# The opening's last block, the plan of the weight forms and the ring of x forms in a fused attention and two-layer MoE kernel

## The chip, the cores and the metric

One core of one Trainium2 chip. The metric is device microseconds of one execution of the whole kernel. The matrix engine (PE in the profile) multiplies 128x128 tiles by 384 columns; VectorE is DVE, ScalarE is ACT, GpSimd is POOL, and SP issues nearly all DMAs.

## What is computed

A linear attention without softmax, a feed-forward layer with ELU, and a mixture of four ReLU experts weighted by given probabilities, all in float32:

```python
kv = einsum('bhsd,bhse->bhde', k, v); o = einsum('bhsd,bhde->bhse', q, kv)
x = o / sqrt(mean(o*o) + 1e-6) * g_norm          # (2304 tokens, 512)
h = x @ w_in                                     # (2304, 2048)
x = where(h > 0, h, exp(min(h, 0)) - 1) @ w_out  # (2304, 512)
out = sum_e p[:, e] * (relu(x @ w1[e]) @ w2[e])  # 4 experts, 512 -> 1024 -> 512
```

w_in and w_out arrive as float64 words. Every product is made of three matmuls of a high and a low part (hi*hi, hi*lo, lo*hi), so each operand must be split first: ACT casts the high part (L194, L321, L266, L638), and POOL or DVE subtracts it from the source for the low part (`split_lo` at L182, `finish_low` at L269).

## The kernel before, in words

The 2304 tokens are six blocks of 384 (`T`), numbered j = 0 to 5. d_ff of layer one is cut into 16 chunks in five groups (`first_groups`): chunks 0-1, 2-3, 4-7, 8-11, 12-15.

**Opening.** Attention and the first group (chunks 0 and 1) are planned by `at_place(place, op)`; the operations are sorted by place, and `in_program_order` (L796) fixes that order on PE, DVE, ACT and POOL. Per block there are two `product1` (x by w_in, 12 matmuls each, into PSUM banks a and b), `begin_elu` (ACT, L490-L491), `end_elu` (DVE, L495), `split_h` (ACT L194, POOL L191), then `half(j, ms)` (L529: x by w_out for two of the four output tiles m, 12 matmuls, into banks e and f) and `half_acc` (two ACT copies, L505, into the accumulator). The halves of block j-1 are placed inside block j; those of the last block stand alone at z = 120 to 123 (L867-L871).

**Rest of layer one.** 84 steps (one per group, block and chunk) run in a pipeline of half-steps, `hh`: on an even one `product1` of step s, then pending accumulations, `split_h` of step s-1 and the planned work of that half-step; on an odd one `emit_mm2` of step s-2 (`LAG = 2`, L1015; 12 matmuls), `begin_elu` and `end_elu` of step s, with the planned work between. For the first two odd half-steps there is no `emit_mm2`. Here the order is fixed on DVE, ACT and POOL alone; PE's is the scheduler's. In each group the weights of the next are converted from float64 and split. Their tiles come from the pools `w` (6 buffers) and `wl` (10 buffers of 4 KB per partition, L91).

**Weight forms.** Layer two multiplies by a scheme of seven products of half-size blocks (P1 to P7), so every quarter of an expert's weights is turned into seven forms, each split in two and written to DRAM (`keptw`) to be streamed later. For one quarter, `make_w` (L252) loads four blocks (b11 to b22), makes four sums on DVE (t1 to t4, L261) and seven splits: ACT cast (L266), one tick later the low part (L271, POOL, or DVE for the names in `late["on_vector"]`), one tick later the write by SP. Each form holds a 4 KB tile from the ring `f` from its sum or cast until the write has landed. Sixteen quarters exist; twelve are made in layer one. `plan_forms` (L292) puts each at half-step offsets out of `FORMS_SLOW` (L288, a new quarter every 16 half-steps, the first six from half-step 28) and `FORMS_FAST` (every 7, six more from half-step 124). From half-step 127 (L1011) P2 and P7 go to DVE, and the ring `f` takes its tiles in turn from its own pool `wf` (4 buffers, L984) and from `wl`: four and three of every seven. The last group begins at half-step 120. In it also the x forms of block pair 0 are made (half-steps 141 to 170).

**Layer two.** Three pairs of blocks by four experts are twelve moves of 14 slots. A slot is one unit of the first product ("q", PSUM qa/qb) of this move and one of the second ("m", ma/mb) of the move before, 12 matmuls each; a q unit reads one weight form and one x form. `evict_q` (L598) takes a q result away: u = ps + P1 (L604, DVE) after P3, for example, without which P5 can't reuse bank qb. A pair needs seven x forms, [128, 2, 2, 384] high and low, made by `make_forms` (L314) in eight calls: two sums; A11; S2; A12 and a sum; S1; S4 and a sum; S3; A22. Each form is an ACT cast (L321) and a tick later its low part (L191, in two pieces on POOL for A11, A12, S4 and A22; on DVE for S2, S1 and S3 of pairs 1 and 2). A form is read twice in a move: in the order A11, S2, A12, S1, S4, S3, A22 at slots 0 to 6 and again at slots 7 to 13. The eight calls for the next pair are made at slots 8 to 15 of a pair's last move (L1070; slot 14 is the next move's first). Forms lie two to a tile of pool `x` (4 buffers); a tile is taken anew for every two forms (`new_form`, L306). The sums take two tiles of pool `s` (16 buffers), which layer two uses for all its intermediate results.

Of the kernel before, what the change touches and what calls it, by code (L numbers as in the profile page):

```python
# [9 lines left out]
F32R = mybir.dt.float32r  # L10
# [23 lines left out]
def attention_moe_kernel(  # L34
# [15 lines left out]
    P = 128  # L50
# [14 lines left out]
    T = 384  # L65
    TT = T // P
    NB = NT // T
# [19 lines left out]
    layer1, with_x_late, with_wm = ExitStack(), ExitStack(), ExitStack()  # L87
    psum = layer1.enter_context(tc.tile_pool(name="psum", bufs=1, space=bass.MemoryType.PSUM))
    x_p = ctx.enter_context(tc.tile_pool(name="x", bufs=4))
    raw_p = layer1.enter_context(tc.tile_pool(name="raw", bufs=2, side="right"))  # L90
    wl_p = layer1.enter_context(tc.tile_pool(name="wl", bufs=10, side="right"))  # L91
    cv_p = layer1.enter_context(tc.tile_pool(name="cv", bufs=2, side="right"))
    h1_p = layer1.enter_context(tc.tile_pool(name="h1", bufs=4, side="right"))
    e_p = layer1.enter_context(tc.tile_pool(name="e", bufs=2, side="right"))
# [1 line left out]
    late = {"on_vector": ()}  # L96
# [3 lines left out]
    def bank(tags, name):  # L100

        n = turns[tags] = turns.get(tags, -1) + 1
        return psum.tile([P, 512], F32, tag=tags[n % len(tags)], name=name, bufs=1)
# [107 lines left out]
    wf = {}  # L211
# [73 lines left out]
        }  # L285


    FORMS_SLOW = "t1:0 t2:2 P5:3 t3:4 t4:6 P3:7 b12:8 b11:8 P4:9 P7:10 b22:10 P1:11 P2:13 b21:14 P6:15", 16  # L288
    FORMS_FAST = "t1:0 t2:1 P5:2 t3:2 b12:3 b11:3 b22:3 t4:3 P3:4 P4:4 P7:5 P1:5 P2:6 P6:7 b21:8", 7
    FORMS_LATE = "t1:0 t2:4 P5:5 t4:8 P3:9 t3:12 P7:13 b12:14 P4:16 P1:18 P2:20 P6:22 b11:22 b22:25 b21:25", 28  # L290

    def plan_forms(n, at, plan, put):  # L292
        steps = make_w(n)
        for what in plan[0].split():
            name, offset = what.split(":")
            if name[0] != "b" or n + 1 != IN_LAYER1:
                put(at + int(offset), steps[name])
        return at + plan[1]

    F_ORDER = [A_OF[q] for q in Q_ORDER]  # L300
    forms, halves = {}, {}
# [3 lines left out]

    def new_form(p, name):  # L306

        n = F_ORDER.index(name)
        if n % 2 == 0:
            halves[p, n] = x_p.tile([P, 2, 2, 2, T], F32R, tag="x", name="f")  # L310
        forms[p][name] = halves[p, n - n % 2][:, n % 2]
        return forms[p][name]

    def make_forms(p):  # L314
# [40 lines left out]
    at = ExitStack()  # L355
# [114 lines left out]
    banks2 = {}  # L470
# [46 lines left out]
    def emit_mm2(g, j, c):  # L517

        first, last = c == first_groups[g][0], c == first_groups[g][-1]
        if first:  # L520
            banks2[j] = [bank("efghcd", "ps_y")[:, :T] for _ in range(KD)]
        for m, ps in enumerate(banks2[j]):
            product2(ps, j, c, m, first, last)
        if last:
            pending.extend((g, j, m, ps) for m, ps in enumerate(banks2[j]))

    pending = []

    def half(j, ms):  # L529

        if j not in acc:
            new_acc(j, [P, KD, T])
        cs = first_groups[0]
        for m in ms:
            banks2[j, m] = bank("ef", "ps_y")[:, :T]
        for c in cs:
            for m in ms:
                product2(banks2[j, m], j, c, m, c == cs[0], c == cs[-1])
# [225 lines left out]
    def at_place(place, op, *args):  # L764
        plan.append((place, len(plan), op, args))
# [67 lines left out]
    for j in range(NB):  # L833
        z = 20 * j
# [29 lines left out]
    plan_float32(0, 3, 68.9, 71.6, 69, 73.9, 74)  # L864
    plan_float32(1, 2, 100, 100.1, 100.2, 103, 103.1)
    plan_float32(1, 3, 108.9, 109, 109.1, 114, 114.6)
    z = 20 * NB  # L867
    at_place(z, half, NB - 1, (0, 1))
    at_place(z + 1, half_acc, NB - 1, (0, 1))
    at_place(z + 2, half, NB - 1, (2, 3))  # L870
    at_place(z + 3, half_acc, NB - 1, (2, 3))  # L871


    for place, what in ((-31, "k0-1 w1c0 k2-4 q0-2 w1c1"), (-18.5, "k5-8 q3-5 w2c0"), (0, "w2c1 k9-11"), (0.05, "q6-8"),
# [95 lines left out]
    def at_step(hs_, *op):  # L970
        todo.setdefault(hs_, []).append(op)

    for g, cs in list(enumerate(first_groups))[1:]:
        begins = 2 * len(steps)
        for n, j in enumerate(range(NB) if g != 3 else range(NB)[::-1]):
            here = 2 * len(steps)
            if g == 1:
                at_step(here + 2, keep_x, j)
            elif g == 2 and n == 0:
                at_step(here, with_x_late.close)  # L980
                at_step(here, lambda: late.update(
                    b=[(with_wm.enter_context(tc.tile_pool(name="wm", bufs=4, reuse_waits="tile")), "b")] * 2 +
                      [(layer1.enter_context(tc.tile_pool(name="wm2", bufs=2, side="right", reuse_waits="tile")), "b")],
                    f=[(layer1.enter_context(tc.tile_pool(name="wf", bufs=4, side="right", reuse_waits="tile")), "f")],  # L984
                ))
                for b in ("b12", "b11", "b22", "b21"):
                    at_step(here, load_block, 0, b)
            if g >= 2 and n >= 4:
                at_step(here - 4 * len(cs), load_x, j)
            steps += [(g, j, c) for c in cs]  # L990
        length = 2 * len(steps) - begins
        if g + 1 < len(first_groups):
            cs = first_groups[g + 1]
            pieces = [p for i in range(0, len(cs), 2) for p in ((0, cs[i]), (0, cs[i + 1]), (1, cs[i]), (1, cs[i + 1]))]
            for n, row in enumerate(pieces):
                at_step(begins + n * (3 if g == 1 else 6), convert, len(rows))
                rows.append(row)
# [9 lines left out]
        at_step(begins + hh, make_one, forms_of_0)  # L1007
    at = begins - 2 * NB * NF * 2 + 4
    for n in range(IN_LAYER1):
        at = plan_forms(n, at, FORMS_SLOW if n < 6 else FORMS_FAST, lambda hh, step: at_step(hh, *step))  # L1010
    at_step(begins + 7, lambda: late.update(  # L1011
        on_vector=("P2", "P7"), f=[late["f"][0], (wl_p, "w")] * 3 + [late["f"][0]]
    ))

    LAG = 2  # L1015
    for hh in range(2 * (len(steps) + LAG)):
        s, second = divmod(hh, 2)
        if not second:
            if s < len(steps):
                product1(*steps[s][1:])  # L1020
            while pending:
                into_acc(*pending.pop(0))
            if 0 < s <= len(steps):
                split_h(*steps[s - 1][1:], nc.vector if s >= len(steps) - 2 else nc.gpsimd)
            tick(*todo.get(hh, ()))
        else:
            if s >= LAG:
                emit_mm2(*steps[s - LAG])
            if s < len(steps):
                begin_elu(*steps[s][1:])  # L1030
            tick(*todo.get(hh, ()))
            if s < len(steps):
                end_elu(*steps[s][1:])
# [33 lines left out]
    slots = len(M_UNITS)  # L1067
    for n, pair_end in enumerate(range(E, len(moves), E)):
        of_next = make_forms(n + 1)
        for slot in range(8, 16):  # L1070
            starts.setdefault(((pair_end - 1) * slots + slot) * 2 + 1, []).append((make_one, of_next))
    starts[0] = [(load_block, IN_LAYER1, b) for b in ("b12", "b11", "b22", "b21")]
    at = 4
    for n in range(IN_LAYER1, len(quarters)):
        at = plan_forms(n, at, FORMS_LATE, lambda half, step: starts.setdefault(half, []).append(step))
# [83 lines left out]
```

## Time and profile before

| | us |
|---|---|
| median of 3 runs | 1217.87 (1217.45 to 1218.7) |
| the profiled execution, its own time | 1217.92 |
| its span in the trace | 1216.1 |
| PE matmul busy in the span | 1175.8 |
| DVE, POOL, ACT busy | 795.5, 659.5, 587.1 |
| granted PE clock, mean of the span | 0.991 |

The span is 1.8 us shorter than the execution's own time, and that time is 0.05 us above the median. In the trace, time runs from the span's start. The opening ends at about 117 us; layer one then runs to 478 us and layer two to the end. A matmul's row may be longer than the distance to the next, since matmuls are pipelined; the number of matmuls in a stretch tells more than the busy time.

### The profile page before, as it was taken

The page shows a single profiled execution, that of the slowest core. Times are in us where ns is not written, and L with a number is a line of the kernel's source. Part 1 is how long each engine was busy: PE and PEld are TensorE (multiplying, and loading weights), DVE is VectorE, ACT ScalarE, POOL GpSimd, SP SyncE. Part 2 cuts the span into 40 slices and gives each one's busy share as a digit, 9 for nine tenths or more (in the row PEclk, how much of TensorE's full clock was granted, in tenths as well). Part 3 has the DMA queues.
Part 4 walks back from the last instruction along what each step waited for, and adds up shares of the span by engine and source line. Part 5 has one row for each costly group of instructions (what it writes and reads, how often), then busy time and mean ns, then how long its engine had stood idle before and what let it go on. Part 6 is the DMA issues. An engine that isn't in the chain of part 4 may idle for free.

```text
span 1216.1 us, 18927 instructions
## 1 busy us (share of the span) xinstructions
PE 1175.8 (97%) x7039; PEld 1157.4 (95%) x7039; DVE 795.5 (65%) x951; ACT 587.1 (48%) x937; POOL 659.5 (54%) x520
## 2 busy tenths in 40 slices
PE   8898999999999998999999999999999999999997
PEld 8798999999999988999999899999999999999996
DVE  5776896676764676477677956454758564647485
ACT  3666665665655564544444533433335334343432
POOL 1122446767656696576666955354447543544441
PEclk9999999999999999999999989999999999999999
DMA  9942247647678978999999868878887778787873
GB/s 344 351 153 106 88 153 244 211 157 268 221 176 291 351 278 324 324 340 362 314 357 324 308 238 260 274 246 271 253 268 236 244 256 278 245 275 254 265 244 115
DMA packets 112159, 312.22 MB, mean 257 GB/s; under 512 B 19580, under 2 KB 40644, under 8 KB 110532
## 3 DMA queue, kind: packets, MB, share of 16 engines
q1 hardware_dynamic: 107236, 306.30, 74.2%
q10 hardware_dynamic: 4832, 4.72, 1.2%
q8 instruction: 56, 0.92, 0.3%
q14 instruction: 35, 0.29, 0.1%
HBM read 238.06 MB, written 72.91 MB: 256 GB/s over the span
## 4 chain that ended last, share of the span: by engine, by line
PE 52%; DVE 4%; issue 1%; POOL 1%; DMA 1%; ACT 1%; ACTq 0%; DVEq 0%; POOLq 0%
PE ps_qb L576 15%; PE ps_ma L576 14%; PE ps_mb L576 11%; PE ps_qa L576 10%; DMA ws<-keptw 1%; DVE acc L685 1%; DVE m L684 1%; DVE f L191 1%; PE ps_mb L731 0%; POOL c L707 0%; DVE h L191 0%; POOL h L191 0%; DVE h L629 0%; DVE h L628 0%; DVE u L604 0%
## 5 line engine op out<-in xcount | busy, mean ns | idle before, releaser
L191 POOL TENSOR_TENSOR h<-h 128x384 fp32r<-128x384 f32 x232 | 280.2, 1232 | 212.4 <-ACT h L638 206.1
L576 PE MATMUL ps_qb<-f,ws 128*128 128x384 f32 x1152 | 218.7, 338 | 10.6 <-DVE u L604 9.5
L576 PEld LDWEIGHTS ps_qb<-f,ws 128*128 128x128 f32 x1152 | 202.7, 190 | 11.9 <-DVE u L604 10.5
L576 PE MATMUL ps_ma<-h,ws 128*128 128x384 f32 x1080 | 200.0, 335 | 0.8 <-DVE h L191 0.7
L191 POOL TENSOR_TENSOR h<-e,h 128x384 fp32r<-128x384 f32 x91 | 102.9, 1131 | 172.0 <-ACT h L194 160.1
L576 PEld LDWEIGHTS ps_ma<-h,ws 128*128 128x128 f32 x1080 | 187.9, 188 | 1.8 <-DVE h L191 1.0
L576 PE MATMUL ps_mb<-h,ws 128*128 128x384 f32 x936 | 174.3, 337 | 1.6 <-ACT o L738 0.8
L638 ACT CAST h<-h 128x768 fp32r<-128x768 f32 x168 | 139.9, 833 | 72.3 <-PE ps_ma L576 37.2
L576 PEld LDWEIGHTS ps_mb<-h,ws 128*128 128x128 f32 x936 | 165.1, 190 | 2.2 <-issue 1.1
L576 PE MATMUL ps_qa<-f,ws 128*128 128x384 f32 x864 | 163.0, 335 | 1.6 <-DMA ws<-keptw 1.0
L576 PEld LDWEIGHTS ps_qa<-f,ws 128*128 128x128 f32 x864 | 150.7, 188 | 2.5 <-issue 1.6
L481 PE MATMUL ps_h<-x,w 128*128 128x384 f32 x384 | 130.5, 340 | 7.6 <-DVE e L495 7.6
L595 ACT ACTIVATE h<-h 128x768 f32<-128x768 f32 x72 | 61.0, 847 | 152.9 <-DVE h L610 71.9
L514 PE MATMUL ps_y<-h,w 128*128 128x384 f32 x384 | 128.8, 335 | 1.7 <-POOL h L191 1.7
L482 PE MATMUL ps_h<-x,w 128*128 128x384 f32 x384 | 128.9, 336 | 0.4 <-DVE x L457 0.4
L483 PE MATMUL ps_h<-x,w 128*128 128x384 f32 x384 | 129.0, 336 | 0.0
L515 PE MATMUL ps_y<-h,w 128*128 128x384 f32 x384 | 128.6, 335 | 0.1
L513 PE MATMUL ps_y<-h,w 128*128 128x384 f32 x384 | 119.3, 339 | 1.9 <-ACT h L194 1.2
L495 DVE SCALAR_TENSOR_TENSOR e<-e,ps_h 128x384 f32<-128x384 f32 x96 | 52.7, 549 | 81.4 <-ACT e L491 69.8
L271 POOL TENSOR_TENSOR wform<-wform 128x512 fp32r<-128x512 f32 x54 | 80.1, 1490 | 22.4 <-ACT wform L266 14.3
L194 ACT CAST h<-e 128x384 fp32r<-128x384 f32 x96 | 49.0, 511 | 73.3 <-DVE e L495 73.2
L481 PEld LDWEIGHTS ps_h<-x,w 128*128 128x128 f32 x384 | 72.3, 188 | 11.2 <-DVE e L495 11.0
(120 smaller groups left out, 1838.1 us busy)
## 6 DMA issues: line engine op xcount, KB each, us to landing
ws<-keptw SPq DMA_DIRECT2D x336, 512.0 KB, 4.4
keptw<-wform SPq DMA_DIRECT2D x112, 512.0 KB, 4.9
wraw<-in_moe_w_dram SPq DMA_DIRECT2D x64, 256.0 KB, 5.2
keptx<-x SPq DMA_DIRECT2D x6, 1536.0 KB, 6.0
x<-keptx SPq DMA_DIRECT2D x6, 1536.0 KB, 8.1
raw<-in_moe_w_in_dram SPq DMA_DIRECT2D x16, 512.0 KB, 4.1
raw<-in_moe_w_out_dram SPq DMA_DIRECT2D x16, 512.0 KB, 3.7
qkv<-in_k_dram SPq DMA_DIRECT2D x18, 256.0 KB, 5.3
```

What stands on the lines that cost most here:

```text
L191: eng.tensor_tensor(out=l, in0=x, in1=h, op=ALU.subtract)
L271: eng.tensor_tensor(out=f[:, 1].bitcast(F32R), in0=src, in1=f[:, 0], op=ALU.subtract)
L481: nc.tensor.matmul(ps, ah, bh, start=(kk == 0), stop=False)
L482: nc.tensor.matmul(ps, ah, bl, start=False, stop=False)
L483: nc.tensor.matmul(ps, al, bh, start=False, stop=(kk == KD - 1))
L495: nc.vector.scalar_tensor_tensor(out=e, in0=e, scalar=-1.0, in1=ps_h.pop((j, c)), op0=ALU.add, op1=ALU.max)
L513: nc.tensor.matmul(ps, bh[:, cols], hi, start=first, stop=False)
L514: nc.tensor.matmul(ps, bh[:, cols], lo, start=False, stop=False)
L515: nc.tensor.matmul(ps, bl[:, cols], hi, start=False, stop=last)
L576: nc.tensor.matmul(ps[:, c, :T], a, x[:, b, kk, :], start=start and kk == 0 and n == 0, stop=stop and kk == 1 and n == 2, skip_group_check ...
L595: nc.scalar.activation(src, src, AF.Relu)
L638: nc.scalar.copy(f[:, 0], src)
```

## The change

The halves of block 5 leave the opening's plan and are issued at half-steps 1 and 3 of the pipeline, where no `emit_mm2` stands; their accumulations go through the pending list of half-steps 2 and 4. Pool `wl` has 9 buffers instead of 10, `wf` 5 instead of 4. Seven quarters follow the slow plan, now one every 13 half-steps (from 28, 41, ... 106), and five the fast plan, now one every 8 (from 119, 127, 135, 143, 151); offsets inside a quarter change with it. From half-step 127 five of every eight tiles of ring `f` are from `wf`. The x forms of all pairs lie in one ring of eight half tiles, and the eight calls for a next pair are made at slots 5, 6, 8, 10, 12, 14, 15 and 17.

```diff
--- before.py
+++ after.py
@@ -88,7 +88,7 @@
     psum = layer1.enter_context(tc.tile_pool(name="psum", bufs=1, space=bass.MemoryType.PSUM))
     x_p = ctx.enter_context(tc.tile_pool(name="x", bufs=4))
     raw_p = layer1.enter_context(tc.tile_pool(name="raw", bufs=2, side="right"))
-    wl_p = layer1.enter_context(tc.tile_pool(name="wl", bufs=10, side="right"))
+    wl_p = layer1.enter_context(tc.tile_pool(name="wl", bufs=9, side="right"))
     cv_p = layer1.enter_context(tc.tile_pool(name="cv", bufs=2, side="right"))
     h1_p = layer1.enter_context(tc.tile_pool(name="h1", bufs=4, side="right"))
     e_p = layer1.enter_context(tc.tile_pool(name="e", bufs=2, side="right"))
@@ -285,8 +285,8 @@
         }
 
 
-    FORMS_SLOW = "t1:0 t2:2 P5:3 t3:4 t4:6 P3:7 b12:8 b11:8 P4:9 P7:10 b22:10 P1:11 P2:13 b21:14 P6:15", 16
-    FORMS_FAST = "t1:0 t2:1 P5:2 t3:2 b12:3 b11:3 b22:3 t4:3 P3:4 P4:4 P7:5 P1:5 P2:6 P6:7 b21:8", 7
+    FORMS_SLOW = "t1:0 t2:2 P5:3 t3:4 t4:5 P3:6 b12:7 b11:7 P4:7 P7:8 P1:9 b22:9 P2:10 P6:11 b21:12", 13
+    FORMS_FAST = "t1:0 t2:1 P5:2 t3:2 b12:3 b11:3 b22:3 t4:3 P3:4 P4:5 P7:6 P1:7 P2:8 P6:9 b21:9", 8
     FORMS_LATE = "t1:0 t2:4 P5:5 t4:8 P3:9 t3:12 P7:13 b12:14 P4:16 P1:18 P2:20 P6:22 b11:22 b22:25 b21:25", 28
 
     def plan_forms(n, at, plan, put):
@@ -305,10 +305,10 @@
 
     def new_form(p, name):
 
-        n = F_ORDER.index(name)
-        if n % 2 == 0:
-            halves[p, n] = x_p.tile([P, 2, 2, 2, T], F32R, tag="x", name="f")
-        forms[p][name] = halves[p, n - n % 2][:, n % 2]
+        n = (len(F_ORDER) * p + F_ORDER.index(name)) % 8
+        if n // 2 not in halves:
+            halves[n // 2] = x_p.tile([P, 2, 2, 2, T], F32R, tag="x", name="f")
+        forms[p][name] = halves[n // 2][:, n % 2]
         return forms[p][name]
 
     def make_forms(p):
@@ -864,11 +864,6 @@
     plan_float32(0, 3, 68.9, 71.6, 69, 73.9, 74)
     plan_float32(1, 2, 100, 100.1, 100.2, 103, 103.1)
     plan_float32(1, 3, 108.9, 109, 109.1, 114, 114.6)
-    z = 20 * NB
-    at_place(z, half, NB - 1, (0, 1))
-    at_place(z + 1, half_acc, NB - 1, (0, 1))
-    at_place(z + 2, half, NB - 1, (2, 3))
-    at_place(z + 3, half_acc, NB - 1, (2, 3))
 
 
     for place, what in ((-31, "k0-1 w1c0 k2-4 q0-2 w1c1"), (-18.5, "k5-8 q3-5 w2c0"), (0, "w2c1 k9-11"), (0.05, "q6-8"),
@@ -981,7 +976,7 @@
                 at_step(here, lambda: late.update(
                     b=[(with_wm.enter_context(tc.tile_pool(name="wm", bufs=4, reuse_waits="tile")), "b")] * 2 +
                       [(layer1.enter_context(tc.tile_pool(name="wm2", bufs=2, side="right", reuse_waits="tile")), "b")],
-                    f=[(layer1.enter_context(tc.tile_pool(name="wf", bufs=4, side="right", reuse_waits="tile")), "f")],
+                    f=[(layer1.enter_context(tc.tile_pool(name="wf", bufs=5, side="right", reuse_waits="tile")), "f")],
                 ))
                 for b in ("b12", "b11", "b22", "b21"):
                     at_step(here, load_block, 0, b)
@@ -1007,9 +1002,9 @@
         at_step(begins + hh, make_one, forms_of_0)
     at = begins - 2 * NB * NF * 2 + 4
     for n in range(IN_LAYER1):
-        at = plan_forms(n, at, FORMS_SLOW if n < 6 else FORMS_FAST, lambda hh, step: at_step(hh, *step))
+        at = plan_forms(n, at, FORMS_SLOW if n < 7 else FORMS_FAST, lambda hh, step: at_step(hh, *step))
     at_step(begins + 7, lambda: late.update(
-        on_vector=("P2", "P7"), f=[late["f"][0], (wl_p, "w")] * 3 + [late["f"][0]]
+        on_vector=("P2", "P7"), f=[late["f"][0], (wl_p, "w")] * 3 + [late["f"][0]] * 2
     ))
 
     LAG = 2
@@ -1026,6 +1021,10 @@
         else:
             if s >= LAG:
                 emit_mm2(*steps[s - LAG])
+            else:
+                ms = (2 * s, 2 * s + 1)
+                half(NB - 1, ms)
+                pending.extend((0, NB - 1, m, banks2.pop((NB - 1, m))) for m in ms)
             if s < len(steps):
                 begin_elu(*steps[s][1:])
             tick(*todo.get(hh, ()))
@@ -1067,7 +1066,7 @@
     slots = len(M_UNITS)
     for n, pair_end in enumerate(range(E, len(moves), E)):
         of_next = make_forms(n + 1)
-        for slot in range(8, 16):
+        for slot in (5, 6, 8, 10, 12, 14, 15, 17):
             starts.setdefault(((pair_end - 1) * slots + slot) * 2 + 1, []).append((make_one, of_next))
     starts[0] = [(load_block, IN_LAYER1, b) for b in ("b12", "b11", "b22", "b21")]
     at = 4
```

## Rows read from the trace of the kernel before

**Rows 1.** The page's busy times: engine, us, share of the span, instructions.
```profile
PE 1175.8 (97%) x7039; PEld 1157.4 (95%) x7039; DVE 795.5 (65%) x951; ACT 587.1 (48%) x937; POOL 659.5 (54%) x520
```
**Rows 2.** Windows: stretch, length, busy us and count per engine, PEclk, DMA share, GB/s.
```profile
120.00:150.00 30.00, 30.00 (x166) 30.00 (x165) 26.61 (x41) 18.43 (x36) 14.28 (x12) 0.94 0.30 89
...
180.00:210.00 30.00, 30.00 (x175) 30.00 (x174) 20.39 (x30) 18.84 (x36) 20.25 (x16) 1.00 0.74 268
...
390.00:420.00 30.00, 27.73 (x157) 26.70 (x156) 20.48 (x33) 15.29 (x32) 18.68 (x16) 1.00 0.97 336
420.00:450.00 30.00, 28.16 (x158) 26.82 (x157) 23.20 (x27) 19.07 (x38) 28.30 (x22) 1.00 0.86 308
450.00:480.00 30.00, 26.15 (x142) 24.23 (x141) 20.64 (x26) 15.86 (x31) 26.86 (x21) 1.00 0.82 303
...
690.00:720.00 30.00, 24.81 (x130) 24.45 (x129) 22.12 (x19) 10.77 (x15) 20.78 (x15) 0.89 0.63 222
...
930.00:960.00 30.00, 26.35 (x143) 26.03 (x142) 23.60 (x21) 12.80 (x17) 20.36 (x14) 0.94 0.65 222
```
**Rows 3.** Timeline of PE where the opening ends: start, us, instruction, idle before.
```profile
116.76 0.34 PE L515 MATMUL ps_y<-h,w 128*128 128x384 f32 x1
119.28 0.45 PE L481 MATMUL ps_h<-x,w 128*128 128x384 f32 x1 [2.17 <-DVE e L495]
```
**Rows 4.** Windows: the 4.7 us after that gap.
```profile
119.30:124.00 4.70, 4.70 (x18) 4.70 (x19) 4.45 (x7) 2.91 (x7) 1.49 (x2) 0.64 0.41 115
```
**Rows 5.** Timeline of ACT ahead of that gap's end.
```profile
113.02 0.62 ACT L194 CAST w<-m 128x512 fp32r<-128x512 f32 x1 [1.52 <-DVE m L179]
...
116.61 1.00 ACT L505 COPY acc<-ps_y 128x384 f32<-128x384 f32 x2 [1.40 <-PE ps_y L515]
117.51 0.50 ACT L490 ACTIVATE e<-ps_h 128x384 f32<-128x384 f32 x1
```
**Rows 6.** Waits of DVE from 385 to 480 us: total, times, longest.
```profile
DVE wform L261 <- DMA keptw<-wform: 9.9, 6, 3.0
```
**Rows 7.** The same wait of DVE from 185 to 385 us.
```profile
DVE wform L261 <- DMA keptw<-wform: 0.7, 1, 0.7
```
**Rows 8.** Groups of POOL from 420 to 480 us: weight forms' low parts.
```profile
L271 POOL TENSOR_TENSOR wform<-wform 128x512 fp32r<-128x512 f32 x10 | 15.4, 1547 | 0.0
L271 POOL TENSOR_TENSOR wform<-wraw,wform 128x512 fp32r<-128x512 f32 x8 | 13.1, 1646 | 0.0
```
**Rows 9.** The page's DMA issues: count, KB each, median us to landing.
```profile
keptw<-wform SPq DMA_DIRECT2D x112, 512.0 KB, 4.9
```
**Rows 10.** Waits of PE from 385 to 480 us.
```profile
PE ps_y L514 <- POOL h L191: 1.7, 3, 0.9
PE ps_y L513 <- ACT h L194: 1.2, 2, 0.9
```
**Rows 11.** Timeline of PE at the two changes of pair.
```profile
694.13 2.24 PE L576 MATMUL ps_qa<-f,ws 128*128 128x384 f32 x12
701.56 4.21 PE L576 MATMUL ps_qb<-f,ws 128*128 128x384 f32 x12 [5.19 <-DVE u L604]
...
944.70 3.00 PE L576 MATMUL ps_qb<-f,ws 128*128 128x384 f32 x12 [3.65 <-DVE u L604]
```
**Rows 12.** Timeline of DVE ahead of the first of them.
```profile
684.22 2.58 DVE L684 TENSOR_TENSOR m<-c,p 128x768 f32<-128x768 f32 x1 [1.72 <-POOL c L707]
...
698.89 1.75 DVE L191 TENSOR_TENSOR f<-s,f 128x768 fp32r<-128x768 f32 x1
700.57 0.94 DVE L604 TENSOR_TENSOR u<-ps_qb,p 128x768 f32<-128x768 f32 x1
```
**Rows 13.** Instructions on tile s, DVE low parts: ns least, median, most.
```profile
L191 DVE TENSOR_TENSOR f<-s,f x6: 954/1754/1769, 676.6 to 942.0; 128x768 fp32r<-128x768 f32 x6
```
**Rows 14.** Timeline of POOL there: low part of x form A12, two pieces.
```profile
679.18 2.77 POOL L191 TENSOR_TENSOR f<-acc,f 128x384 fp32r<-128x384 f32 x2
```
**Rows 15.** Waits of the whole span: a result's copy behind an x form.
```profile
ACT p L692 <- POOL f L191: 5.6, 2, 3.6
```

## The prediction

> **What bounds the kernel now.** I read the busy times first: PE works 97% of the span and no other engine over 65% [rows 1]. So only time in which PE stands still, or runs at a lower clock, can be won. Next the windows of 30 us [rows 2]. An undisturbed stretch holds 175 matmuls, a pitch of 30 / 175 = 0.171 us, and a half-step or unit of 12 matmuls lasts 2.06 us. A stretch with fewer shows the loss directly, idle time and slow clock together: 166 at 120-150 us, 157 + 158 + 142 at 390-480 us, 130 at 690-720 us and 143 at 930-960 us. The missing matmuls times 0.171 are 1.5, 11.7 (68 of them), 7.7 and 5.5 us. The change touches the code of each of these places, and each must be read for the wait that ends last there.
>
> **The opening's end.** PE stops from 116.76 to 119.28 us [rows 3], 2.35 us over the pitch, until the ELU of pipeline step 0 frees a PSUM bank. In the 4.7 us behind the gap the granted clock averages 0.64 [rows 4], so part of it ran at 1.2 instead of 2.4 GHz: 4.7 x 0.36 = 1.7 us. ACT's order makes this wait: `begin_elu` of step 0 (L490) stands in program order behind both copies of block 5's last half, starts at 117.51, and the copies themselves had waited for PE [rows 5]. The step's own product had long been computed.
>
> The change removes four planned operations and adds the same 48 matmuls and four copies; none of this work disappears. What moves is ACT's order: `begin_elu` of step 0 follows the weight cast that ends at 113.02 + 0.62 = 113.6, ends about 1.0 later, and `end_elu` about 115.2, instead of 119.2. PE has block 5's second half to do until then and step 2's product after it. The second half needs banks e and f, whose copies now follow `begin_elu`: about 0.5 us that PE hadn't lost before. Gain 2.35 + 1.7 - 0.5 = **3.5 us**; bounds 0 (PE's order here is the scheduler's, and the wait could reappear on the copies) and 4.1.
>
> **Layer one's last group, 390-480 us.** Two things are short. First, tiles for forms: DVE waits 9.9 us for a form's write to land, against 0.7 us in the 200 us before [rows 6, 7]. DVE takes instructions in order, so an `end_elu` behind that wait is late and PE's bank with it. Second, POOL is busy 28.3 and 26.9 of 30 us [rows 2], 28.5 of these 55.2 us in 18 low parts of weight forms at 1.58 us [rows 8].
>
> Tiles: in the slow plan four tiles served seven forms per 16 half-steps, a turn of 4/7 x 16 = 9.1 half-steps; with five per 13 it is 9.3. In the fast plan seven tiles in strict rotation gave a turn of 7 half-steps; eight at seven forms per 8 half-steps give 9.1. A form holds its tile for 4 or 5 half-steps and 4.9 us, or 2.4 half-steps, for the write [rows 9], up to 7.4: over 7, under 9.1. So the wait for tiles goes. POOL: the old fast quarters start at 124 to 159, the new ones at 119 to 151. From half-step 143 on (about 425 us) 15 low parts of any engine remain instead of 23, and on POOL 11 instead of 18: 7 x 1.58 = 11.1 us less, 44 instead of 55 us. What remains in the sum are PE's waits on `split_h`, 1.7 + 1.2 us [rows 10], since the x forms of pair 0 still crowd POOL there. Gain 11.7 - 2.9 = **8.8 us**; bounds 0 (POOL still sets the pace) and 11.7.
>
> The work that leaves here goes into half-steps 28 to 119, where PE now loses nothing (the 180 us row, one of seven alike, [rows 2]). POOL has 10 of 30 us free there and gets some 2 more. The narrowest place is P6's cast at offset 11, whose tile is free at 8 + 2.4 = 10.4. I charge 0.5 us; bounds 0 and the opposite rival below. The tenth `wl` buffer costs nothing while weights turn over: the last `wl` tile of a group is cast at half-step 71 of a group whose first is read for the last time at 69, and ACT then stands behind a later PE product anyway. If that cover is gone, ACT waits one unit, 2.06 us, at two group changes. The forms' DMAs keep their number; SP only issues them earlier.
>
> **The two changes of pair.** PE waits 5.19 and 3.65 us for L604, and the clock falls [rows 2, 11]: 7.7 + 5.5 = 13.2 us in all. DVE had no idle time from 684.22 on; L604 itself takes 0.94 us [rows 12]. Ahead of it stand sums, products and the low part of x form S3, 1.75 us [rows 12]. That operation can take 0.954 us, but its median is 1.754 [rows 13]: DVE and POOL hinder each other, POOL being busy without a break.
>
> The Trainium skill ("SBUF — State Buffer", SBUF: two separate sides) says that a DVE instruction with two SBUF inputs and a GpSimd instruction exclude one another for the whole instruction. By that rule spreading wins no port time, it only moves who waits; the row agrees with the exclusion, and the sum by the rule alone would be the lower bound given next.
>
> Of the eight calls S3's now comes one slot later, so its 1.75 us falls behind L604. A12's two POOL pieces, 2.77 us [rows 14], leave the place where POOL's c (L707) kept DVE idle for 1.72 us [rows 12]; I take 1.3 of it. With POOL no longer closed up, two of six slowed DVE operations run at 0.95: 2 x 0.8 = 1.6 us. Sum 4.65 of 5.19, so 0.5 us of idle time stays at the first change and none at the second. Upper end: 7.7 - 0.5 + 5.5 = 12.7 us, with the clock. Lower end: S3's 1.75 us twice, 3.5 us. No row is nearer to one end; I take the middle, **8.1 us**.
>
> Waits that the change adds here: each cast into the ring waits for the last reader of that half tile. By slots, S2 at slot 8 takes the half read at 7, and the later ones have a slot or two more; nothing queues behind them. The sums' two `s` tiles are held from slot 5 to 15 instead of 8 to 14. Counted in program order, up to 15 of 16 tiles are live at slots 5 to 8, where 12 or 13 were; the peak of 16 is there before and after. Such a shortage shows today as ACT's 5.6 us behind POOL [rows 15]; it belongs to the bounds.
>
> **Sum.** 3.5 + 8.8 + 8.1 - 0.5 = 19.9 us off the profiled execution's 1217.92, which lies 0.05 above the median: 1198.0 us. A measurement can tell 0.2%, 2.4 us, from no change.
>
> **Rivals.**
> *A, the pair changes keep their stall.* S4, S3 and A22 are now made at slots 14, 15 and 17, in the same crowd; DVE still works off 17 us of queue. For it: DVE and POOL busy without a break there. Against it: three x operations fewer on DVE from slot 8 on. 1198.0 + 8.1 = 1206.1 us.
> *B, the last group keeps its loss,* because POOL, at 44 us plus lengthening by DVE, still sets the pace. Against it: 390-420 us lost 18 matmuls with POOL at only 18.7 us. 1206.8 us. *A and B together:* 1214.9 us.
> *C, slower: the tiles run short in the slow stretch.* P6's spare time falls from 1.6 half-steps (offset 15 against 11 + 2.4) to 0.6, 1.2 us. Once a write lands more than that late, ACT, and `begin_elu` behind its cast, waits; past some 4 us (two banks ahead) PE stops. Priced as the fast plan's 390-420 us: 18 x 0.171 = 3.1 us per 30 us, over 91 half-steps or 187 us 19.2 us, and the last group wins nothing: 1217.9 - 3.5 - 8.1 + 19.2 = 1225.5 us. Against it: the turn grows from 9.1 to 9.3, and DMAs are 0.74 busy there [rows 2].
> *D, the opening doesn't do what it says:* the scheduler sets PE's order so that the wait stays. 1201.5 us.
>
> **Chances.** Forecast 0.54, A 0.14, B 0.12, both 0.07, C 0.09, D 0.04. Faster: forecast, A, B and D, 0.84; same: A and B together, 0.07; slower: C, 0.09. The range takes in the forecast with its bounds, D, A and B with some spread, and leaves out A with B, C and the best corner: 1190 to 1211 us.
>
> **What would show it.** Opening: no gap over 1 us between 113 and 122 us and the clock at 1.00. Last group: over 170 matmuls per 30 us, DVE's wait on `keptw` under 2 us, POOL under 24 of 30 us. Pair changes: PE's waits on L604 under 1 us each, 165 or more matmuls in those 30 us. Wrong would be new waits of ACT casts on `keptw` between 190 and 360 us, fewer than 173 matmuls there, or waits of q units on POOL's f four to six slots into a new pair.

## The result and the profile after

| | us |
|---|---|
| the changed kernel, median of 4 runs | 1202.83 (1199.56 to 1203.93) |
| the kernel before beside it, median of 4 | 1218.28 (1217.45 to 1220.69) |
| ratio after / before | 0.9866, interval [0.9841, 0.989] |
| the profiled execution: own time, span, mean clock | 1203.93, 1202.1, 0.993 |

Faster by 1.3%: 16 us by the ratio, 15.5 between the medians, where 19.9 was forecast; 1202.83 lies in the range, above its middle. The change works, but two of the four terms are clearly not of the size forecast, and a third is right in its sum and not in its parts. (After line 867 the changed kernel's line numbers are 5 lower; in e7 to e10, which are made from it, they are 7 higher from line 250 on to the end of the opening's plan, so L604 is L611, L495 is L502 and L481 is L488 there.)

To give the gain a place I cut the span at fixed points of the work: starts of `end_elu` (L495) on block 5's first chunk and on steps 8, 59 and 63 of the pipeline, and of the L604s around each change of pair. DVE's timeline of the changed kernel at these cuts:

```profile
107.13 0.55 DVE L495 SCALAR_TENSOR_TENSOR e<-e,ps_h 128x384 f32<-128x384 f32 x1 [1.70 <-ACT e L491]
...
153.78 0.55 DVE L495 SCALAR_TENSOR_TENSOR e<-e,ps_h 128x384 f32<-128x384 f32 x1
...
364.69 0.55 DVE L495 SCALAR_TENSOR_TENSOR e<-e,ps_h 128x384 f32<-128x384 f32 x1 [1.49 <-ACT e L491]
...
379.77 0.55 DVE L495 SCALAR_TENSOR_TENSOR e<-e,ps_h 128x384 f32<-128x384 f32 x1
...
478.35 0.96 DVE L604 TENSOR_TENSOR u<-ps_qb,p 128x768 f32<-128x768 f32 x1 [4.18 <-PE ps_qb L576]
...
657.66 0.96 DVE L604 TENSOR_TENSOR u<-ps_qb,p 128x768 f32<-128x768 f32 x1
...
720.75 0.96 DVE L604 TENSOR_TENSOR u<-ps_qb,p 128x768 f32<-128x768 f32 x1 [3.66 <-PE ps_qb L576]
...
870.48 0.95 DVE L604 TENSOR_TENSOR u<-ps_qb,p 128x768 f32<-128x768 f32 x1
...
958.18 0.96 DVE L604 TENSOR_TENSOR u<-ps_qb,p 128x768 f32<-128x768 f32 x1 [3.72 <-PE ps_qb L576]
```

The differences between cuts, for every profile of this study (us); "last group" runs from step 63 to layer two's first L604. The first profiled execution of e3 was a slow one, 2204.52 us at a granted clock of 0.871, so its stretches are read from a second run.

| kernel | opening's end | slow stretch | last group | pair change 1 | pair change 2 |
|---|---|---|---|---|---|
| before | 47.8 | 210.7 | 104.5 | 67.0 | 92.2 |
| **after** | 46.6 | 210.9 | 98.6 | 63.1 | 87.7 |
| e1 opening alone | 44.9 | 210.7 | 105.1 | 67.0 | 93.1 |
| e2 weight forms alone | 49.8 | 210.9 | 98.5 | 66.1 | 92.2 |
| e3 x forms alone (second run) | 48.0 | 210.7 | 105.3 | 63.1 | 87.7 |
| e4 ring alone | 47.9 | 210.7 | 104.0 | 66.1 | 92.2 |
| e5 plans alone | 47.8 | 212.5 | 99.7 | 66.8 | 93.1 |
| e6 pools alone | 49.4 | 210.4 | 101.1 | 66.6 | 92.2 |
| e11 one `wl` buffer less | 49.9 | 210.4 | 104.3 | 66.9 | 93.2 |
| e7 after, loads held | 44.9 | 210.9 | 98.3 | 63.1 | 87.7 |
| e8 e7 and S3 later | 44.8 | 210.9 | 98.2 | 59.8 | 86.7 |
| e9 e7 and pair 0 later | 45.0 | 210.9 | 95.4 | 63.1 | 87.7 |
| e10 e8 and e9 | 44.8 | 210.9 | 95.2 | 59.9 | 86.7 |

A stretch that an edit doesn't touch repeats to about 1 us, most of them to 0.2 (the first change of pair shows 66.1 us in e2, which leaves the x forms alone, and the second 93.1 in e1 and e5). Before to after: -1.1, +0.2, -5.9, -3.9, -4.5, and -0.5 between steps 59 and 63; the untouched rest gives -0.1, and the start of the first stretch, which no edit of the change reaches and which lies anywhere from 104.6 to 107.8 us in these profiles, came 1.7 later. Together -14.0, the difference of the two spans; it is less than 15.5 because the profiled execution of after lies 1.1 us above its median and that of before 0.4 below.

The windows of after, columns as in [rows 2]:

```profile
120.00:150.00 30.00, 30.00 (x172) 29.51 (x171) 25.46 (x40) 19.11 (x38) 13.47 (x12) 1.00 0.29 89
180.00:210.00 30.00, 30.00 (x175) 30.00 (x174) 24.52 (x32) 19.56 (x38) 22.71 (x17) 1.00 0.82 295
390.00:420.00 30.00, 28.11 (x161) 27.41 (x160) 21.59 (x31) 16.34 (x34) 20.88 (x17) 1.00 0.89 325
420.00:450.00 30.00, 29.22 (x167) 28.56 (x166) 22.43 (x27) 19.85 (x39) 28.36 (x23) 1.00 0.71 255
450.00:480.00 30.00, 28.95 (x166) 28.31 (x165) 13.39 (x22) 11.37 (x21) 15.18 (x13) 1.00 0.63 224
690.00:720.00 30.00, 27.65 (x153) 27.30 (x152) 18.10 (x17) 13.48 (x17) 19.20 (x16) 0.94 0.80 268
930.00:960.00 30.00, 29.24 (x170) 28.89 (x170) 17.85 (x18) 13.63 (x17) 18.43 (x17) 1.00 0.83 273
```

Every stretch of [rows 2] that had lost matmuls holds more, the 180 us row is still full, but 390 to 480 us has 31 missing of 525, and 690 to 720 still shows 0.94. PE's waits over the whole span, one of before and two of after: the wait on L604 fell from 9.5 us to 3.7.

```profile
PE ps_qb L576 <- DVE u L604: 9.5, 3, 5.2
```

```profile
PE ps_h L481 <- DVE e L495: 5.4, 6, 1.9
PE ps_qb L576 <- DVE u L604: 3.7, 3, 2.3
```

The opening shows what the prediction had not looked for. A timeline of all engines in the changed kernel:

```profile
98.42 1.94 SPq L248 DMA_DIRECT2D wraw<-in_moe_w_dram  x4
...
100.86 0.34 SPq L903 DMA_DIRECT2D keptx<-x  x1
...
104.73 0.34 SPq L138 DMA_DIRECT2D raw<-in_moe_w_out_dram  x1
...
110.19 0.43 DVE L151 TENSOR_SCALAR x<-raw 128x512 uint32<-128x512 uint32 x1 [2.50 <-DMA raw<-in_moe_w_out_dram]
...
113.16 0.56 DVE L495 SCALAR_TENSOR_TENSOR e<-e,ps_h 128x384 f32<-128x384 f32 x1 [1.49 <-ACT e L491]
...
113.77 0.44 PE L481 MATMUL ps_h<-x,w 128*128 128x384 f32 x1 [1.86 <-DVE e L495]
```

The gap of [rows 3] is gone from its place. But four loads of 256 KB for the first weight forms, which the kernel before issues at 161.41 us, now stand ahead of `keptx` and of the raw w_out load in SP's queue. The raw load is issued no later, 2.40 us ahead of block 5's first `end_elu` as before, but it takes 5.4 us to land, where the kernel before has 3.6 in the median of these loads. DVE waits 2.50 us for it, in order, and the `end_elu` behind it (113.16) is late for PE.

### The profile page after: what moved, and what is told of

Same layout as the page of the kernel before. It is cut to its first block, busy times and chain, and to the rows that moved or that the text cites. A ratio compares the mean times of both kernels' runs of the same rounds, so it can differ in the third digit from the quotient of the medians.

```text
span 1202.1 us, 18910 instructions
## 1 busy us (share of the span) xinstructions
PE 1171.6 (97%) x7039; PEld 1155.4 (96%) x7039; DVE 799.6 (67%) x948; ACT 587.8 (49%) x937; POOL 672.1 (56%) x523
## 4 chain that ended last, share of the span: by engine, by line
PE 54%; DVE 3%; issue 1%; DMA 1%; ACT 0%; POOL 0%; ACTq 0%; DVEq 0%; POOLq 0%
PE ps_qb L576 15%; PE ps_ma L576 15%; PE ps_mb L576 12%; PE ps_qa L576 11%; DMA ws<-keptw 1%; DVE acc L685 1%; DVE m L684 0%; PE ps_mb L731 0%; DVE h L629 0%; DVE h L191 0%; DVE u L604 0%; DVE h L628 0%; POOL c L707 0%; DVE u L704 0%; DVE f L191 0%
## 5 line engine op out<-in xcount | busy, mean ns | idle before, releaser
L191 POOL TENSOR_TENSOR h<-h 128x384 fp32r<-128x384 f32 x232 | 284.0, 1250 | 204.9 <-ACT h L638 199.6
L191 POOL TENSOR_TENSOR h<-e,h 128x384 fp32r<-128x384 f32 x91 | 105.3, 1158 | 151.6 <-ACT h L194 137.1
L481 PE MATMUL ps_h<-x,w 128*128 128x384 f32 x384 | 129.9, 338 | 5.5 <-DVE e L495 5.4
L514 PE MATMUL ps_y<-h,w 128*128 128x384 f32 x384 | 129.6, 337 | 1.1 <-POOL h L191 1.0
L515 PE MATMUL ps_y<-h,w 128*128 128x384 f32 x384 | 129.4, 337 | 0.0
L513 PE MATMUL ps_y<-h,w 128*128 128x384 f32 x384 | 123.2, 339 | 1.9 <-ACT w L194 1.9
L495 DVE SCALAR_TENSOR_TENSOR e<-e,ps_h 128x384 f32<-128x384 f32 x96 | 52.6, 549 | 69.7 <-ACT e L491 66.9
L194 ACT CAST h<-e 128x384 fp32r<-128x384 f32 x96 | 49.0, 511 | 66.8 <-DVE e L495 66.7
L481 PEld LDWEIGHTS ps_h<-x,w 128*128 128x128 f32 x384 | 72.1, 188 | 8.4 <-DVE e L495 8.3
```

Of the source, the lines that this page charges most:

```text
L191: eng.tensor_tensor(out=l, in0=x, in1=h, op=ALU.subtract)
L481: nc.tensor.matmul(ps, ah, bh, start=(kk == 0), stop=False)
L495: nc.vector.scalar_tensor_tensor(out=e, in0=e, scalar=-1.0, in1=ps_h.pop((j, c)), op0=ALU.add, op1=ALU.max)
L513: nc.tensor.matmul(ps, bh[:, cols], hi, start=first, stop=False)
L514: nc.tensor.matmul(ps, bh[:, cols], lo, start=False, stop=False)
L515: nc.tensor.matmul(ps, bl[:, cols], hi, start=False, stop=last)
```

## Experiments

**The three parts by themselves.** Each is the kernel before with some hunks of the diff; code is shortened here and below, with "..." for what is left out. First the opening alone:

```diff
-    at_place(z, half, NB - 1, (0, 1))
...
+            else:
+                ms = (2 * s, 2 * s + 1)
+                half(NB - 1, ms)
```

> The kernel before with the opening's part alone (block 5's halves in half-steps 1 and 3). Theory: the part is worth the 3.5 us of the prediction when nothing else is in its way; in the changed kernel it showed less because four loads of expert weights (wraw), issued at 98 us instead of 161 us, lay ahead of a load of w_out, and this kernel's DMA order has them late as before. So -3 to -4 us against the kernel before, no wait of DVE over 1 us on a raw load between 100 and 115 us, PE without a gap over 1 us from 113 to 122 us. Rival: the gain is given back by DVE, which is busy 28 of 30 us from 150 us on; then the halves move but the times at layer two's start stay within 1 us, 0 to -1 us.

1215.68 us, ratio 0.998 [0.997, 0.9991]: 2.4 us faster by the ratio, less than the 3 to 4 expected. The opening's end fell by 2.9 us; DVE's wait on the raw load is 0.7 us and PE's longest gap there 0.62, so the conditions of the theory hold and its size doesn't quite.

The weight forms alone (pools, plans, the list of ring f):

```diff
-    wl_p = ... bufs=10
+    wl_p = ... bufs=9
-    FORMS_SLOW = ... 16
+    FORMS_SLOW = ... 13
```

> The kernel before with the pools (wl 9, wf 5, ring f five of eight) and the two plans of weight forms alone. Theory: layer one's last group gains 6 to 9 us, and the opening loses about 2 us, since the same four wraw loads are issued early here too (they follow from the pools or the plan, not from the opening's part): -4 to -7 us in all, with a wait of DVE of 2 us or more on a raw load near 107 us. Rival: the early loads cost nothing and the gain is the whole 8.8 us of the prediction or the 6 us that the changed kernel shows from 380 to 478 us: -6 to -9 us and no such wait.

1213.5 us, 0.9966 [0.9953, 0.998]: 4.1 us. The last group gave 6.0 and the opening took 2.0 back, with a wait of DVE of 2.6 us on the raw load, so the early loads come with this part.

The x forms alone (`new_form` and the slots of the next pair):

```diff
-        for slot in range(8, 16):
+        for slot in (5, 6, 8, 10, 12, 14, 15, 17):
```

> The kernel before with the ring of half slots and the new slots alone. Theory: the two changes of pair gain 8 us (3.9 and 4.6 in the changed kernel), whatever layer one does, since the queues are empty in between: -7.5 to -9 us. Rival: part of it came from the weight forms' new plan, which ends earlier: then -4 us or less.

> The kernel before with the ring and the new slots alone, once more for an undisturbed profile. If the gain of 8.4 us lies where the prediction put it, the stretches over the changes of pair are about 63.1 and 87.7 us as in the changed kernel (67.0 and 92.2 before), with the opening (47.8), the slow stretch (210.7) and the last group (104.5) as before; if the gain at the pair changes depends on the earlier edits, they are over 64 and 89 us.

1209.2 us, 0.9931 [0.9918, 0.9944]: 8.4 us. The profile of the second run has just the stretches of after at both changes, 63.1 and 87.7. The three parts make 2.4 + 4.1 + 8.4 = 14.9 us of the 16: within the intervals they add.

**The loads held back.** The changed kernel, with the first four of these loads ordered behind the opening's last w_in load on SP:

```diff
+        if n == 0:
+            tc.add_manual_dep(i, late["sp"].name, ...)
```

> The changed kernel, with the first four wraw loads held behind the opening's last load of w_in in SP's order; nothing else differs on any engine. Theory: DVE's wait of 2.5 us on w_out's load at 107 us and PE's of 1.9 us at 113.8 us go, and 1.5 to 3 us of the opening's gain come back: about -2 us against the changed kernel, -17.5 against the kernel before. Rival: the load is late because of the 1.5 MB write of x ahead of it, as slow before, and nothing changes beyond 0.5 us.

1200.32 us, 0.9857 [0.9841, 0.9873]. The loads go out at 111.20 and what DVE waited falls from 2.50 to 0.73 us:

```profile
102.19 0.33 SPq L138 DMA_DIRECT2D raw<-in_moe_w_out_dram  x1
...
105.87 0.43 DVE L151 TENSOR_SCALAR x<-raw 128x512 uint32<-128x512 uint32 x1 [0.73 <-DMA raw<-in_moe_w_out_dram]
...
111.20 1.96 SPq L248 DMA_DIRECT2D wraw<-in_moe_w_dram  x4
```

The opening's end gains the 2.9 us of e1, and the time is 2.5 us below after between the medians, about 2 being expected. Only SP's order was edited: the loss of 1.8 us in after's opening is the queue's order.

**Which half of the weight forms' part does what.** Plans without pools, pools without plans, and one pool by itself:

```diff
+    FORMS_SLOW = ... 13      (e5)
+    wl bufs=9, wf bufs=5     (e6)
+    wl bufs=9                (e11)
```

> The kernel before with the new paces and offsets of the weight forms alone (seven quarters every 13 half-steps, five every 8); the pools keep 10 and 4 buffers, so the ring of forms still has seven tiles in the last group and four before. In the last group the kernel before takes 104.5 us from the end of the slow plan to layer two's first L604, and the changed one 98.6 us. Theory A (fewer low parts late, so POOL and DVE are freed by the paces): the plan alone gives most of it, 99 to 100.5 us, total 1213 to 1214.5 us. Theory B (tiles are what was short): with seven tiles the wait of DVE for a form's write stays near 9 us and the stretch stays above 102.5 us, and with four tiles at one quarter per 13 half-steps, a turn of 4/7 x 13 = 7.4 half-steps, the slow stretch (210.7 us) loses too: total 1217 us or above.

1214.76 us, 0.9964 [0.995, 0.9977]. Both theories hold in part: the last group and the total come out about as A has them, and what B said of the waits and of the slow stretch is there too. By the cuts the last group falls by 4.8 us and the slow stretch grows by 1.9; but these cuts are starts on DVE, which is itself late at step 59 here. PE lost 5 matmuls in the slow stretch, 0.9 us, so that 4.8 - 1.0 = 3.8 us are the last group's, with DVE's wait on `keptw` there as long as before, 10.8 us. And the slow stretch does run short of tiles: ACT's casts wait, the longest 3.6 us at 307, just ahead of PE's loss. The waits of ACT from 185 to 385 us, and the window, in e5:

```profile
ACT wform L266 <- DMA keptw<-wform: 7.7, 3, 3.6
```

```profile
300.00:330.00 30.00, 29.54 (x170) 29.22 (x169) 21.20 (x30) 18.21 (x36) 20.99 (x18) 1.00 0.72 245
```

In after that wait is 1.1 us, behind 370 us, and every window from 180 to 360 us is full: the fifth `wf` buffer, the one difference of the two in the ring of forms there, pays for the faster pace.

> The kernel before with the pools alone changed (nine and five buffers for ten and four, five of every eight late tiles of ring f from wf); paces and offsets of the old plans. In SP's order the first four weight blocks (L248) stand early here, as in the changed kernel, and late in the other parts. Theory (the early loads are a side effect of the pools): from block 5's first to step 8's end_elu this kernel takes about 2 us more than before (47.8), as the weight-form part did, with DVE waiting over 2 us for the raw w_out load; if instead the paces cause it, the stretch stays at 47.8. In the last group the tiles for a turn go from 7 to 8 half-steps while the low parts stay as crowded: if tiles alone were short, the stretch falls from 104.5 to about 100 us; if POOL's crowd also counts, to about 102.5. Total 1215 to 1218 us.

1217.6 us, 0.9996 [0.9987, 1.0005]. The last group falls by 3.3 us to 101.1 us, between the 100 expected if tiles alone were short and the 102.5 if POOL's crowd also counts, and no wait on `keptw` is left in it; the opening loses 1.7 to the early loads. Tiles alone and paces alone give 3.3 and 3.8, both together 6.0: they overlap a little.

> The kernel before with one edit: wl has nine buffers instead of ten. It asks which part of the pools edit moves the first four weight blocks, and what that buffer is worth by itself. Theory (the tenth buffer is what kept those loads back, and costs nothing else): SP issues the four loads (L248) near 98 us instead of 161, DVE waits over 2 us for the raw w_out load, the stretch from block 5's first to step 8's end_elu is 49.4 to 49.8 us instead of 47.8, every later stretch is as before; total 1218.5 to 1220.5 us. Rival (the five wf buffers move them): the loads stay at 161 us and the stretch at 47.8. Second rival (weights of layer one turn over more slowly with nine): the slow stretch (210.7 us) or the last group (104.5 us) is longer by over 0.5 us.

1221.03 us, 1.002 [1.0011, 1.003]: slower by 0.2%, a little more than expected. One buffer of `wl` less sends the four loads out at 99.11 instead of 161.41 us, and the opening's end takes 2.1 us more; the other stretches stay within 0.3, but for 1.1 at the second change of pair, which e1 and e5 show too.

```profile
99.11 1.93 SPq L248 DMA_DIRECT2D wraw<-in_moe_w_dram  x4
...
105.42 0.34 SPq L138 DMA_DIRECT2D raw<-in_moe_w_out_dram  x1
```

Why that buffer had kept the loads back in the scheduler's order was not tried.

**The ring without the new slots.**

```diff
-            halves[p, n] = x_p.tile(...)
+            halves[n // 2] = x_p.tile(...)
```

> The kernel before with the ring of eight half tiles alone; the eight calls for the next pair stay at slots 8 to 15. Theory (spacing the calls is what helps, the ring only makes it possible): the stretches over the changes of pair stay within 0.5 us of 67.0 and 92.2 us, total 1217 to 1219 us. Rival (waiting for a whole tile of two forms was part of the stall): one or both stretches fall by 1 us or more, total 1216 us or below.

1217.83 us, 1.0001 [0.999, 1.0011]: nothing. The first change of pair fell by 0.9 us, over the 0.5 allowed, but it did so in e2 as well, with the old forms; PE's 8.8 us of waits on L604 at the two changes are as before. The ring makes the earlier slots possible; the slots give the gain.

**What is left at the changes of pair.** DVE ahead of L604 in the changed kernel, to be read against [rows 12]:

```profile
677.50 2.60 DVE L684 TENSOR_TENSOR m<-c,p 128x768 f32<-128x768 f32 x1 [1.74 <-POOL c L707]
...
687.11 1.76 DVE L327 TENSOR_TENSOR s<-acc 128x768 f32<-128x768 f32 x1
...
692.16 0.94 DVE L604 TENSOR_TENSOR u<-ps_qb,p 128x768 f32<-128x768 f32 x1
```

S3's low part has moved behind L604, but its sum (687.11) stands ahead of it, in a row without a break. Experiment, on e7:

```diff
-        for slot in (5, 6, 8, 10, 12, 14, 15, 17):
+        for slot in (5, 6, 8, 10, 12, 15, 16, 17):
```

> The held kernel (1200.3 us) with the third x form from the end, S3, and its sum made one and two slots later: slots 15, 16, 17 for the last three calls where 14, 15, 17 stood. In the changed kernel a sum of 1.76 us (L327) still stood on DVE ahead of L604 at the first change of pair, where PE waited 2.35 us, and 0.76 us at the second. Theory (what stands ahead of L604 on DVE sets that wait): with the sum behind L604 the wait falls to about 0.6 us at the first change and to none at the second; the stretch between the L604s on either side of the changes falls from 63.1 and 87.7 us to about 61.5 and 87; total 1198 to 1199 us. Rival (POOL sets it): POOL works without a break from 671 to 695 us, L604 stays where it is because DVE waits for POOL's c instead, and the forms made last come late for the q unit that reads them first, a new wait of PE on POOL's f; 63.1 us or more at the first change, total 1200 us or above.

1195.46 us, 0.9807 [0.9795, 0.982]. The theory's mechanism holds and its price was too small. PE in the changed kernel, then in e8:

```profile
688.56 2.24 PE L576 MATMUL ps_qa<-f,ws 128*128 128x384 f32 x12
693.16 3.91 PE L576 MATMUL ps_qb<-f,ws 128*128 128x384 f32 x12 [2.35 <-DVE u L604]
...
932.15 2.38 PE L576 MATMUL ps_qb<-f,ws 128*128 128x384 f32 x12 [0.76 <-DVE u L604]
```

```profile
687.13 2.35 PE L583 MATMUL ps_qb<-f,ws 128*128 128x384 f32 x12 [0.65 <-DVE u L611]
```

```profile
690.00:720.00 30.00, 30.00 (x177) 29.96 (x177) 17.54 (x16) 13.33 (x17) 18.71 (x16) 1.00 0.82 279
```

The wait falls by 1.70 us, and the window that had granted 0.94 grants 1.00: 30 x 0.06 = 1.8 us of clock that I had left out of the expectation. Together 3.5, and the stretch fell by 3.3; at the second change the wait of 0.76 us is gone and the stretch falls by 1.0. From 640 to 960 us PE waits for nothing else: no new wait on POOL's f took its place.

**What is left in the last group.** On e7, the x forms of pair 0 made later:

```diff
-    for hh in (21, 25, 26, 33, 34, 41, 42, 50):
+    for hh in (30, 34, 36, 39, 41, 44, 47, 50):
```

> The held kernel (1200.3 us) with the x forms of block pair 0 made at offsets 30, 34, 36, 39, 41, 44, 47, 50 of layer one's last group, where 21, 25, 26, 33, 34, 41, 42, 50 stood. POOL was busy 28.4 of the 30 us from 420 to 450 and the last group still lost 31 of 525 matmuls from 390 to 480 us. Theory (POOL's crowd in 420 to 450 us delays h and e tiles, and that is what is left of the loss there): POOL falls below 25 of 30 us there, ACT's wait for the e tile behind POOL falls from 6.0 to under 3 us, and the stretch from the end of the slow plan to layer two's first L604 falls from 98.3 to about 96 us; total about 1198 us. Rival (the weights' loads and the forms' writes set the pace, with DMA 0.89 busy from 390 to 420 us): the stretch stays within 0.5 us of 98.3. Second rival: the crowd only moves to 450 to 480 us, where POOL had 15 of 30 us, and layer two starts late: 99 us or more.

1197.13 us, 0.9818 [0.9803, 0.9832]. The stretch falls by 3.0 us, as the theory had it, though POOL is still 27.0 of 30 us busy, where under 25 was expected. The windows of e9:

```profile
390.00:420.00 30.00, 28.91 (x167) 28.52 (x166) 20.89 (x29) 17.22 (x37) 22.94 (x18) 1.00 0.94 336
420.00:450.00 30.00, 30.00 (x175) 30.00 (x174) 20.89 (x27) 20.43 (x39) 27.03 (x21) 1.00 0.74 274
450.00:480.00 30.00, 29.47 (x171) 29.15 (x170) 12.13 (x19) 10.43 (x18) 13.22 (x13) 1.00 0.62 206
```

Waits from 385 to 480 us, first of after, then of e9 (e7, whose work lies some 4 us earlier, has the three of after at 9.7, 6.0 and 5.1 us):

```profile
DVE wform L261 <- DMA wraw<-in_moe_w_dram: 10.1, 3, 5.9
ACT e L490 <- POOL h L191: 6.0, 3, 2.5
DVE wform L261 <- DMA keptw<-wform: 5.1, 1, 5.1
```

```profile
DVE wform L268 <- DMA wraw<-in_moe_w_dram: 7.1, 3, 5.8
DVE wform L268 <- DMA keptw<-wform: 5.2, 1, 5.2
```

In e9 ACT no longer waits for an e tile behind POOL's low parts of h, while 12.3 of DVE's 15.2 us of waits for blocks and tiles of forms are still there, and PE loses 12 of 525 matmuls instead of 31 in after and 32 in e7. So the long waits in the list were not most of what PE lost: at most the 12 matmuls that are left, 2.1 us, can be theirs. The place of the x forms was. That it acts through POOL is argued from the wait of ACT that vanished; the edit also moves the forms' casts on ACT and their sums on DVE, and no run tells these apart.

> Both edits at once, the later S3 and the later x forms of pair 0, on the held kernel. They lie 200 us apart on different waits, so each theory expects the sum of the two single runs, to within 0.5 us: about 1196 us if both theories hold, 1200.3 us if neither does.

1192.94 us, 0.9787 [0.9774, 0.98], the best of the study: every stretch is that of the single edit. The medians add less well (7.4 us below e7, where the singles gave 4.9 and 3.2), with four to five runs each that spread by up to 4 us.

## Why the prediction was nearly right, point by point

*The opening, 3.5 us forecast.* The mechanism was right: `begin_elu` came ahead of the copies, and the gap with its low clock went. Alone it measures 2.9; a wait of some 0.6 us stays at the same place, on `end_elu` and not, as charged, on the copies. In the change it nets 1.1, because two statements about the weight forms were wrong: that the tenth `wl` buffer costs nothing, and that SP only issues the forms' DMAs earlier. I looked for the buffer's price at the changes of group. It lay in SP's queue, where e11 shows it at 2.1 us and e7 wins back 1.8. Condition "no gap over 1 us": missed, 1.86.

*The last group, 8.8 us forecast, 5.9 measured.* The count was right. Eleven low parts on POOL from 420 to 480 us, 43.5 us of POOL time in all, 11 and 44 foreseen:

```profile
L271 POOL TENSOR_TENSOR wform<-wform 128x512 fp32r<-128x512 f32 x6 | 9.1, 1531 | 0.0
...
L271 POOL TENSOR_TENSOR wform<-wraw,wform 128x512 fp32r<-128x512 f32 x5 | 7.8, 1561 | 0.0
```

"Over 170 matmuls per 30 us" was missed (161, 167 and 166). What failed is the remainder that I left in: "1.7 + 1.2 us", PE's waits on `split_h` read from before. They are down to 1.0; but POOL's time didn't fall evenly. 28.4 us of it lie in 420 to 450, as in before and against the condition of under 24, since the x forms of pair 0 kept their half-steps. ACT's e tiles wait for POOL there, 6.0 us [the list under e9], a path to PE that the sum had left out. Moving those x forms gives 3.0 us in e9, the missing part. "DVE's wait on `keptw` under 2 us" failed as well (5.1); e9 keeps that wait, and still gains its 3.0 us.

*The changes of pair, 8.1 forecast, 3.9 + 4.5 = 8.4 measured.* The sum is right, its parts are not. S3's 1.75 us left the queue: from the start of L684 to that of L604 were 16.35 us in [rows 12] and are 14.66 now. The c of L707 came earlier against PE: L684 starts 11.06 us ahead of the qa unit's matmuls, against 694.13 - 684.22 = 9.91 [rows 11, 12], a gain of 1.15 where 1.3 was taken. 1.69 + 1.15 = 2.84, which is 5.19 - 2.35. The 1.6 us for "two of six slowed DVE operations" never came. DVE's slowed rows between L684 and L604, before, beside the two of [rows 12]:

```profile
686.73 1.77 DVE L191 TENSOR_TENSOR f<-s,f 128x768 fp32r<-128x768 f32 x1
...
690.15 2.05 DVE L327 TENSOR_TENSOR s<-acc 128x768 f32<-128x768 f32 x1
...
693.86 1.77 DVE L684 TENSOR_TENSOR m<-c,p 128x768 f32<-128x768 f32 x1
695.55 1.75 DVE L629 TENSOR_TENSOR h<-h 128x768 f32<-128x768 f32 x1
697.23 1.74 DVE L685 TENSOR_TENSOR acc<-acc,m 128x768 f32<-128x768 f32 x1
```

After, beside the rows of 677.50 and 687.11 above, with one row of POOL:

```profile
677.43 1.84 POOL L616 TENSOR_TENSOR h<-u,p 128x768 f32<-128x768 f32 x1
...
680.02 1.77 DVE L191 TENSOR_TENSOR f<-s,f 128x768 fp32r<-128x768 f32 x1
...
685.42 1.76 DVE L684 TENSOR_TENSOR m<-c,p 128x768 f32<-128x768 f32 x1
...
688.79 1.77 DVE L629 TENSOR_TENSOR h<-h 128x768 f32<-128x768 f32 x1
690.49 1.75 DVE L685 TENSOR_TENSOR acc<-acc,m 128x768 f32<-128x768 f32 x1
```

Of seven slowed rows S3's is gone, and none of the other six runs at 0.95. The Trainium skill (SBUF — State Buffer, SBUF: two separate sides) has a DVE instruction with two SBUF inputs and a GpSimd instruction that reads SBUF exclude one another for the whole instruction. The trace agrees: L684 at 677.50 begins 0.07 us behind POOL's L616 and ends 0.83 us behind its end, so that it seems to have stood still for nearly all of it. While POOL has work without a break, as here up to 694.84 us, spreading its work shortens nothing, and I should have followed that; S3's low part, which now comes at 695.58, takes 0.94 us. At the second change the same two terms were enough to bring the wait from 3.65 to 0.76 us, and the clock came back from 0.94 to 1.00 [rows 2]. That 8.1 met 8.4 is in part luck: it was the middle between 3.5 and 12.7 us, taken because no row was nearer to one end, and not the sum of these terms.

*The slow stretch, -0.5 forecast, -0.2 measured*; rival C did not come about, nor its sign, a wait of ACT's casts on `keptw` between 190 and 360 us. e5 shows that its mechanism is real: with four tiles at the new pace ACT waits on `keptw`, and PE loses 0.9 us. My price for it, 19.2 us, was far too high: I let every quarter run short, and even with four tiles one did up to 370 us.

Rivals A and B each named a whole term as lost. A did not come about; of the last group a third of the term was lost, and for B's reason, POOL, as far as e9 can be read so. Nor did D: alone, the opening's wait falls to 0.6 us. The forecast is 4.8 us below the result: 2.4 in the opening, 2.9 in the last group, less what the other terms gave.

## What to carry to other kernels

When a buffer count changes, read the DMA queue's order around the first tiles of every pool that may move, not only the waits of the pool itself. A queue of 17 us on an in-order engine ahead of a critical eviction is shortened by what can be moved behind that eviction, one operation at a time, and the last piece can be worth more than its length when the clock comes back with it. And the longest wait in a list need not be the one that PE loses to: move the suspected work and see.

## What was not expected of the hardware

How much of a gap's price is clock. At the first change of pair PE stood for 2.35 us and the 30 us window behind shows 0.94, so part of it ran at 1.2 instead of 2.4 GHz: 1.8 us more. With 0.65 us there (e8), and with 0.76 us at the second change, the window shows 1.00 and nothing is added; nor is it behind the 1.86 us at 113.77 us in after, where the clock stays at 1.00. In [rows 2, 11] the gaps were 5.19 and 3.65 us with 0.89 and 0.94.
